# Attention into soft mixture of experts: v and x turned on VectorE, logits by slot, combine in 32-row tiles

## The chip, the core and the metric

The kernel runs on one core of a Trainium2 chip. Time is device time of one execution in microseconds. The core has a matrix engine (PE in the profile), a vector engine (DVE), a scalar engine (ACT), GpSimd (POOL) and a sync engine (SP) that only starts transfers here. Every load of this kernel is started by POOL, every store by SP. Loads read f32 from device memory and write bf16 to on-chip memory (SBUF). Products land in PSUM, eight banks of 512 f32 per partition.

## What is computed

```
q, k, v: 4 batches x 8 heads x 768 positions x 64        (f32)
scores = q @ k.T / 8; causal; heads that are not "retrieval" keep only
         the last 64 positions and the first 4
attn   = softmax(scores) @ v
x      = attn as 3072 tokens x 512 (heads side by side)
logits = x @ phi                        # 3072 x 32 slots, 8 experts of 4 slots
d      = softmax of logits over tokens;  slot_in = d.T @ x        # 32 x 512
per expert e: slot_out = relu(slot_in[e] @ w1[e]) @ w2[e]         # 512 -> 1024 -> 512
c      = softmax of logits over slots;   out = c @ slot_out       # 3072 x 512
```

## The kernel before, in words

Every step is an operation with a rough cost, a priority, dependencies and buffers. A planner (`Plan`) places them by these and then writes each engine's list in that order. On the chip each engine works through its list in order; an instruction that waits holds what stands behind it. POOL's list holds the issues of all loads (`dma`) and the operation VF, so these follow each other.

The 16 pairs of heads (n and n+4 of a batch, four pairs a batch, T = 6.2 us apart in the plan) go through this:

- Loads. `load_part` brings q, k and v of a batch into slots of 8 KB per partition, eleven of them (`S8`), which the expert weights share. Batch 0 comes in three parts per tensor, two of them in 2 KB runs; the others in 8 KB runs. `load_w` brings 16 weights of 1 MB in bf16; the last five go to memory of the attention that has become free (`late_mem`).
- Turns of q, k, v. PE transposes raw chunks into PSUM (lines 415, 439, 461) and DVE or ACT copies them to SBUF (`copy`, lines 218 and 220), so that head dimension lies on partitions. v is turned a second time, back to positions on partitions (V2, line 524, then VB).
- VF (line 541, on POOL): the first four blocks of v times the flag of the head, for score blocks that only retrieval heads keep.
- QK (line 488) in five groups of 1024 columns per pair plus one extra block (QX); exponentials EX on ACT (line 562, pT has two buffers, two pairs); masks MK on DVE (lines 500, 505, 507) for three groups.
- PV (line 621) into one PSUM tile: 42 products of 65 columns a pair, the 65th column being the row sum. From the third block of rows on it reads VF's result.
- NM on DVE (lines 633, 635) divides by the row sum and writes x. PE transposes x (XT, line 647) for the logits, which are taken per token (LG, line 662): 24 products of 32 columns a batch. EL (line 676) is their exponential on ACT.
- DS (line 684) sums x by slot, SA adds the batches up. TE and EE (lines 711, 720) turn the exponentials into expT, four copies of the slots on 128 partitions, for the combine.

After the last pair a chain follows: the last XT, LG, EL, DS, SA; SI (line 768) brings the slot inputs into shape; H (line 781) is the first expert layer, four experts side by side in column tiles of 32; relu (HR), transposes (TH), copies (HE); W2 (line 825) is the second layer, 128 products of 256 columns in tiles of 32, four abreast; CS (line 751) sums the exponentials over tokens by 96 one-column products, RC inverts; SO scales; then 24 tiles of 128 tokens: OM (line 887), a copy with scale by the row sum on ACT or DVE (lines 894, 896), and stores.

Of the kernel before, what the change touches and what calls it, by code (L numbers as in the profile page):

```python
# [10 lines left out]
F32 = mybir.dt.float32  # L11
BF16 = mybir.dt.bfloat16
I32 = mybir.dt.int32
ALU = mybir.AluOpType
# [111 lines left out]
def kernel(  # L126
# [26 lines left out]

    slots = [sb.tile([P, 8 * KB], BF16, name=f"slot{i}") for i in range(11)]
    qk_mem = [sb.tile([P, 12 * KB], BF16, name=f"qk{i}") for i in range(2)]
    pt_mem = sb.tile([P, 20 * KB], BF16, name="pt")
    vx_mem = [sb.tile([P, 3168 + 1024], BF16, name=f"vx{i}") for i in range(2)]
    xv_mem = sb.tile([P, 9 * 1024], BF16, name="xv")
    vfs = [sb.tile([P, 2, 4, 66], BF16, name=f"vf{i}") for i in range(3)]
    ptx = [m[:, 3168:4192].rearrange("p (i n c) -> p i n c", i=2, n=4) for m in vx_mem]  # L160
    xbs = [xv_mem[:, 6144 * i:6144 * i + 3072].rearrange("p (j c) -> p j c", j=6) for i in range(2)]
    xT = sb.tile([P, 4, 768], BF16, name="xT")
    msk = sb.tile([P, H, 640], BF16, name="msk")
    expT = sb.tile([P, 4, 768], BF16, name="expT")
    elg = sb.tile([P, B, 6, NS], BF16, name="elg")
    fm = sb.tile([P, H, 4], BF16, name="fm")
    ident = sb.tile([P, P], BF16, name="ident")
    phf = sb.tile([P, 4, NS], F32, name="phf")
    phi = sb.tile([P, 4, NS], BF16, name="phi")
# [4 lines left out]
    emask = sb.tile([P, 2], F32, name="emask")  # L174
    rcs = sb.tile([P, 1], F32, name="rcs")
    cols = sb.tile([P, 2], BF16, name="cols")
# [4 lines left out]
    edist = sb.tile([P, 640], BF16, name="edist")  # L181
# [3 lines left out]
    vT = xv_mem[:, 3072:6144].rearrange("p (x c) -> p x c", c=128)  # L185
    vbs = [m[:, 0:3168].rearrange("p (n b i d) -> p n b i d", n=4, b=6, i=2) for m in vx_mem]

    tq = xT[:, 0:2, 0:256].bitcast(F32)
    tq = xT.rearrange("p a c -> p (a c)")[:, 0:512].bitcast(F32)
    td = xT.rearrange("p a c -> p (a c)")[:, 512:1024].bitcast(F32)  # L190
    tn = xT.rearrange("p a c -> p (a c)")[:, 1024:1536].bitcast(F32)
    jrow = xT.rearrange("p a c -> p (a c)")[:, 1536:1792].bitcast(F32)
    rne = xT.rearrange("p a c -> p (a c)")[:, 1792:1824].bitcast(F32)
# [8 lines left out]

# [5 lines left out]
    xbf = xT.rearrange("p a c -> p (a c)")  # L208
    hT_t = [xbf[:, 1024 * e:1024 * (e + 1)].rearrange("p (f c) -> p f c", f=8) for e in range(2)]

    pl = Plan({"S8": 11, "QT": 2, "KT": 2, "VT": 1, "VB": 2, "VF": 3, "PT": 2, "PTX": 2, "XB": 2,
               "XT": 1, "SC": 2, "TR": 2, "PV": 1})
    T = 6.2
# [8 lines left out]

    def dma(name, key, nbytes, ndesc, buf, dst, src, deps=()):
        iss = pl.op("issue " + name, {"POOL": 0.62}, key, deps=deps, acq=[buf] if buf else [],
                    emit=lambda o: nc.gpsimd.dma_start(dst(), src))  # L225
        took = ndesc / 16 * 0.0225 + nbytes / 16 / 27170.0
        return pl.op("land " + name, {"DMA": took}, key, deps=[iss], lead=iss_lead[0])

    iss_lead = [2.3]
    raws, lands = {}, {}  # L230
    srcs = {"q": q, "k": k, "v": v}

    def raw_view(buf, p0, p1):
        return slots[buf.slot][p0:p1, :].rearrange("p (i x) -> p i x", i=2)

    def raw_src(x, b, n0, n1):
        a = srcs[x][b].rearrange("(i n) (t s) d -> n t i (s d)", i=2, s=32)[n0:n1]
        return a.rearrange("n t i x -> (n t) i x")


    seq = []
    raw_rel = {}

    def load_part(x, b, part, key):
        if part is None:
            buf = Buf("S8")
            raws[x, b] = buf
            lands[x, b, None] = dma(f"{x}{b}", key, 96 * 2 * 8192, 192, buf,
                                    lambda: raw_view(buf, 0, 96), raw_src(x, b, 0, 4))
        elif part < 2:  # L250
            if (x, b, "s") not in raws:
                raws[x, b, "s"] = Buf("S8")
            buf = raws[x, b, "s"]
            a = srcs[x][b].rearrange("(i n) (t s) d -> n t i (s d)", i=2, s=8)[part]
            lands[x, b, part] = dma(f"{x}{b}.{part}", key, 192 * 2048, 192, buf if part == 0 else None,
                                    lambda: short_view(buf, part), a)
        else:
            raws[x, b] = buf = Buf("S8")
            lands[x, b, part] = dma(f"{x}{b}.{part}", key, 96 * 8192, 96, buf,
                                    lambda: raw_view(buf, 0, 48), raw_src(x, b, 2, 4))  # L260

    def short_view(buf, part):
        return slots[buf.slot][0:96, 1024 * part:1024 * (part + 1)].rearrange("p (i x) -> p i x", i=2)
# [10 lines left out]
    def load_w(i, key, deps=()):  # L274
        if i < NE:
            src = moe_w1[i].rearrange("(di do) f -> di do f", do=4)
        else:
            src = moe_w2[i - NE].rearrange("(fi fo) d -> fi fo d", fo=8)
        wland[i] = dma(f"w{i}", key, 2 << 20, 128, None if i in late_mem else wbuf[i],
                       lambda: w_view(i), src, deps=deps)  # L280


    def tables(o):
        nc.gpsimd.iota(jrow, [[1, 128]], base=0, channel_multiplier=0, allow_small_or_imprecise_dtypes=True)
        nc.gpsimd.iota(pc_i[:, 0:1], [[0, 1]], base=0, channel_multiplier=1)
        nc.gpsimd.iota(tq, [[128, 2], [1, 32], [32, 4]], base=0, channel_multiplier=0,
                       allow_small_or_imprecise_dtypes=True)
# [5 lines left out]
    def key_pos(o):  # L293
        nc.vector.tensor_scalar(pc_i[:, 1:2], pc_i[:, 0:1], 3, 5, op0=ALU.bitwise_and,
                                op1=ALU.logical_shift_left)
        nc.vector.tensor_single_scalar(pc_i[:, 2:3], pc_i[:, 0:1], 2, op=ALU.logical_shift_right)
        nc.vector.tensor_tensor(pc_i[:, 1:2], pc_i[:, 1:2], pc_i[:, 2:3], op=ALU.bitwise_or)
        nc.vector.tensor_copy(pc[:, 1:2], pc_i[:, 1:2])
        nc.vector.tensor_scalar(td, tq, pc[:, 1:2], None, op0=ALU.subtract)
# [3 lines left out]
        nc.vector.tensor_copy(edist[:, 512:640], edist[:, 0:128])  # L303

    def flags(o):
# [3 lines left out]
        nc.vector.tensor_scalar(pc[:, 2:3], pc[:, 1:2], float(n_sink), None, op0=ALU.is_lt)  # L309
# [5 lines left out]
    def head_mask(h):  # L315
        nc.vector.tensor_scalar(msk[:, h, 0:256], edist[:, 0:256], thr[:, 0, h:h + 1], None, op0=ALU.is_lt)
        nc.vector.tensor_scalar(msk[:, h, 256:640], edist[:, 256:640], thr[:, 1, h:h + 1], None, op0=ALU.is_lt)

    def slot_tables(o):

# [4 lines left out]
        nc.vector.tensor_scalar(sum4, jrow[:, 0:NS], pc[:, 3:4], None, op0=ALU.is_equal)  # L325
        nc.vector.tensor_tensor(pc[:, 4:5], pc[:, 4:5], pc[:, 5:6], op=ALU.subtract)
        for e4 in range(2):
            nc.vector.tensor_single_scalar(emask[:, e4:e4 + 1], pc[:, 4:5], 4.0 * e4, op=ALU.is_equal)
        nc.vector.memset(cols[:, 0:1], 1.0)
        nc.vector.memset(cols[:, 1:2], 0.25)  # L330

# [3 lines left out]
    def sp_front(o):  # L335
        nc.sync.dma_start(ri, ri_src)
        pv_ = moe_phi.rearrange("(i n d) s -> i d n s", i=2, n=4)
        for i in range(2):
            nc.sync.dma_start(phf[64 * i:64 * (i + 1)], pv_[i])

    o_sp = pl.op("front", {"SP": 3.5}, -100, emit=sp_front)
    for x in "qk":
        load_part(x, 0, 0, -90)
    o_tab = pl.op("tables", {"POOL": 0.9}, -80, emit=tables)
    load_part("v", 0, 0, -70)
# [606 lines left out]
```

## Time and profile before

| | |
|---|---|
| median of 3 runs | 164.48 us (164.48 to 164.98) |
| span of the profiled execution | 163.6 us, 0.9 below the median |
| PE, PEld busy | 130.3 us (80%), 92.9 us (57%) |
| DVE, ACT busy | 109.4 us (67%), 109.8 us (67%) |
| POOL busy | 39.8 us (24%) |
| loads by POOL (software queue) | 26.22 MB written, 81.2% of 16 engines' span |
| stores by SP (hardware queue) | 6.37 MB, 9.8% |
| last exponential of the attention ends | 122.7 us |
| first product of the first expert layer | 130.1 us |
| first product of the combine | 144.4 us |

PEld is PE loading its stationary operand, which overlaps its products. Issuing a load counts as no busy time on POOL in the shares by engine, though its rows in the order of time have a length. A note in brackets at the end of a row gives the idle time before it and what ended that; "x4" counts instructions that were merged into one row. A group's mean is the time of one instruction from start to end; where instructions overlap, busy time over count is smaller.

### The profile page before, as it was taken

The numbers are of one execution on the slowest core, as the hardware profiler recorded it, in microseconds if no ns is written. First come the engines' busy times: TensorE is split into PE (matmuls) and PEld (weight loads), VectorE is DVE, ScalarE is ACT, GpSimd is POOL, SyncE is SP. The second block draws the span as 40 slices with busy tenths as digits, with TensorE's granted clock in tenths as the row PEclk, the third lists the DMA queues.
The fourth block names the chain that finished last, engine by engine and source line by source line (L and its number), as shares of the span: only waits on it lengthen the run. The fifth ranks groups of instructions, "written<-read, shape, count | busy, mean of one in ns | idle before, by whom it ended". The sixth has DMA issues, their size and how long they took to land.

```text
span 163.6 us, 6186 instructions
## 1 busy us (share of the span) xinstructions
PE 130.3 (80%) x2780; PEld 92.9 (57%) x2780; DVE 109.4 (67%) x228; ACT 109.8 (67%) x133; POOL 39.8 (24%) x59
## 2 busy tenths in 40 slices
PE   0698999999798999988999899699684599978100
PEld 0666777777576676767666676567462246932000
DVE  1899576575787899799799885869975204059400
ACT  3486653288799898898899899979990023068500
POOL 7964311430224202322300243333320000000000
PEclk9999999999999999999999999999998559999955
DMA  2999999999999999999999179999999991019995
GB/s 38 185 197 152 197 210 214 216 218 216 206 216 214 222 220 208 213 211 213 226 215 198 28 118 204 222 218 212 210 222 216 210 216 24 8 62 389 427 423 238
DMA packets 7771, 32.97 MB, mean 201 GB/s; under 512 B 1377, under 2 KB 2529, under 8 KB 5185
## 3 DMA queue, kind: packets, MB, share of 16 engines
q0 software_dynamic: 5760, 26.22, 81.2%
q1 hardware_dynamic: 1984, 6.37, 9.8%
q8 instruction: 21, 0.34, 0.8%
q14 instruction: 6, 0.04, 0.1%
HBM read 52.50 MB, written 6.29 MB: 359 GB/s over the span
## 4 chain that ended last, share of the span: by engine, by line
PE 56%; DVE 15%; ACT 14%; issue 5%; DMA 2%; DVEq 0%; ACTq 0%; POOLq 0%
PE pv L621 15%; PE sc L488 12%; ACT pt L562 10%; PE tr L461 8%; PE sc L781 4%; DVE pt L505 4%; PE tr L439 3%; DVE slot L896 3%; PE tr L647 3%; PE tr L415 2%; DMA slot<-in_q_dram 2%; PE pv L825 2%; DVE xv L635 2%; PE tr L524 2%; PE tr L684 2%
## 5 line engine op out<-in xcount | busy, mean ns | idle before, releaser
L562 ACT ACTIVATE pt<-sc 128x1024 bf16<-128x1024 f32 x80 | 78.7, 1031 | 14.9 <-PE sc L488 13.9
L488 PE MATMUL sc<-qk 64*128 64x256 bf16 (+2 forms) x384 | 35.3, 278 | 3.0 <-ACT pt L562 2.5
L621 PEld LDWEIGHTS <-pt 128*128 128x128 bf16 x640 | 25.4, 101 | 6.9 <-issue 4.8
L621 PE MATMUL pv<-vx,pt 128*128 128x65 bf16 x352 | 28.6, 199 | 0.5 <-DVE pt L507 0.5
L541 POOL TENSOR_TENSOR vf<-vx,fm 128x528 bf16<-128x528 bf16 x16 | 17.8, 1113 | 39.8 <-DVE vx L220 23.6
L621 PE MATMUL pv<-vf,pt 128*128 128x65 bf16 x288 | 23.5, 201 | 0.0
L461 PE MATMUL tr<-ident,slot 96*64 96x96 bf16 x576 | 19.6, 211 | 2.0 <-issue 0.8
L488 PEld LDWEIGHTS <-qk 64*128 64x128 bf16 x384 | 14.0, 97 | 10.6 <-issue 4.6
L461 PEld LDWEIGHTS <-slot 96*64 96x64 bf16 x576 | 15.0, 111 | 6.9 <-issue 5.6
L505 DVE TENSOR_TENSOR pt<-pt,msk 128x512 bf16<-128x512 bf16 x32 | 16.1, 543 | 0.7 <-ACT pt L562 0.6
L635 DVE TENSOR_TENSOR xv<-pv,rs 128x768 bf16<-128x768 f32 x16 | 15.3, 958 | 0.6
L220 DVE COPY qk<-tr 128x768 bf16<-128x768 bf16 x23 | 12.7, 554 | 4.4 <-PE tr L461 3.2
L220 DVE COPY xT<-tr 128x768 bf16<-128x768 bf16 (+1 forms) x15 | 8.6, 573 | 9.4 <-PE tr L804 7.1
L500 DVE TENSOR_TENSOR pt<-pt,msk 128x1024 bf16<-128x1024 bf16 x16 | 11.8, 734 | 2.5 <-ACT pt L562 2.4
L415 PE MATMUL tr<-ident,slot 96*64 96x48 bf16 x192 | 6.9, 228 | 6.6 <-DMA slot<-in_q_dram 5.2
L647 PE MATMUL tr<-ident,xv 128*128 128x128 bf16 x96 | 8.6, 230 | 3.4 <-DVE xv L635 2.4
L225 POOL DMA_DIRECT2D slot<-in_moe_w_dram x11 | 6.3, 573 | 19.7 <-PE tr L461 5.9
L507 DVE TENSOR_TENSOR pt<-pt,msk 128x768 bf16<-128x768 bf16 x16 | 9.4, 587 | 2.2 <-ACT pt L562 1.9
L415 PEld LDWEIGHTS <-slot 96*64 96x64 bf16 x192 | 6.2, 153 | 8.2 <-DMA slot<-in_q_dram 5.2
L647 PEld LDWEIGHTS <-xv 128*128 128x128 bf16 x96 | 6.3, 102 | 5.4 <-DVE xv L635 3.5
L524 PE MATMUL tr<-ident,xv 128*128 128x128 bf16 x96 | 8.6, 232 | 0.4 <-ACT xv L218 0.4
L792 ACT ACTIVATE msk<-sc,emask 128x512 bf16<-128x512 f32 x4 | 2.5, 683 | 7.8 <-PE sc L781 7.8
(106 smaller groups left out, 165.4 us busy)
## 6 DMA issues: line engine op xcount, KB each, us to landing
slot<-in_moe_w_dram POOLq DMA_DIRECT2D x11, 1024.0 KB, 20.6
out_dram<-slot SPq DMA_DIRECT2D x4, 1024.0 KB, 6.9
slot<-in_q_dram POOLq DMA_DIRECT2D x3, 768.0 KB, 30.2
slot<-in_k_dram POOLq DMA_DIRECT2D x3, 768.0 KB, 30.0
slot<-in_v_dram POOLq DMA_DIRECT2D x3, 768.0 KB, 26.2
qk<-in_moe_w_dram POOLq DMA_DIRECT2D x2, 1024.0 KB, 14.9
out_dram<-slot SPq DMA_DIRECT2D x3, 512.0 KB, 3.6
vx<-in_moe_w_dram POOLq DMA_DIRECT2D x1, 1024.0 KB, 15.7
```

Of the source, the lines that this page charges most:

```text
L220: nc.vector.tensor_copy(dst, src)
L415: nc.tensor.matmul(t[64 * i:64 * (i + 1), :, :, s, :], rv[:, i, s, :], idv, start=True, stop=True)
L461: nc.tensor.transpose(t[64 * i:64 * (i + 1), :, s, :], rv[:, i, 8 * c + s, :], ident[0:96, 0:96])
L488: nc.tensor.matmul(scb[sc.slot][:, i, c:c + 128 * nb], kk, qq.rearrange("p b c -> p (b c)"), start=True, stop=True)
L500: nc.vector.tensor_tensor(pT, pT, mh[:, :, 0:512], op=ALU.mult)
L505: nc.vector.tensor_tensor(pv_, pv_, m, op=ALU.mult)
L524: nc.tensor.transpose(t[:, 128 * j:128 * (j + 1)], vT[:, 6 * n + j, :], ident)
L541: eng.tensor_tensor(vfs[VFb[p].slot], vv, mm, op=ALU.mult)
L562: nc.scalar.activation(pTs[PTb[b, n].slot][:, :, 512 * g:512 * (g + 1)], scb[sc.slot], ACT.Exp, scale=scale)
L621: nc.tensor.matmul(pvb[:, h, 65 * i:65 * (i + 1)], lt, rhs, start=(j == 0), stop=(j == i))
L635: nc.vector.tensor_tensor(xo, pvw[:, :, :, 0:64], r.rearrange("p i (j o) -> p i j o", o=1).to_broadcast([P, 2, 6, 64]), op=ALU.mult)
L647: nc.tensor.transpose(t[:, 128 * i:128 * (i + 1)], xv[:, i, 128 * n:128 * (n + 1)], ident)
```

## The change

- v: PE's two turns and their copies go. v is loaded in six pieces (`load_v`), each by four transfers of 32 partitions (or four for two pieces together), and one DVE block transpose per piece (VT, 1024 f32 words per partition, each word two neighbouring bf16) writes it with positions on partitions. VF reads that. v of all batches stays in one memory (`vn`).
- q and k of batch 0 come in two halves of 8 KB runs instead of three parts. q's order within a block of 128 positions changes to match v's; k's copies to SBUF become strided.
- x: PE's turn and its copy become one DVE block transpose per pair (XT, 384 f32 words).
- Logits: taken by slot. phi is laid out as 16 stationary matrices of 128 x 128 with phi's values on diagonal blocks; LG is 16 products of 192 columns a batch. The exponential eT has slots on partitions and gives its own sum over tokens; a DVE transpose (EK) makes the form for DS. TE, EE and the 96 products of CS go; CS is one product.
- Masks: `msk` is 768 columns a head instead of 640, so that each MK is one instruction.
- Experts: HE is four copies per group of four experts, each spreading one expert's 32 columns over 128. W2 becomes 64 products of 512 columns on the full array, so that the slot outputs lie four times, on each 32 partitions. OM uses row tiles of 32 partitions of eT.
- Row sums: six products of 4 columns instead of 24 of one.
- Late weights: 12 and 14 go to the two halves of `vn`, 11 and 13 to q/k memory, 15 to x's memory in three transfers. Weights 14 and 15 wait for the last PV and the last DS. The plan's spacing T is 5.6, and loads, weights and pieces of v are listed in a new order.

```diff
-        lands[x, b, None] = dma(f"{x}{b}", key, 96 * 2 * 8192, 192, buf,
-                                lambda: raw_view(buf, 0, 96), raw_src(x, b, 0, 4))
+    vsrc = v.rearrange("b h (a r s) d -> (b h a) r (s d)", r=4, s=32)
+    def load_v(m, nm, key):
...
+        for r in range(4):
+            src = vsrc[32 * m:32 * (m + nm), r].rearrange("(m g) x -> g m x", m=nm)
+            ls.append(dma(f"v{m}.{r}", key, nm * 32 * 8192, 32 * nm, buf if first and r == 0 else None,
...
-    load_w(0, -30)
-    batch_loads(1, -29)
-    load_w(1, -28)
-    load_w(2, -27)
-    batch_loads(2, -26)
-    for i in (3, 4, 5):
-        load_w(i, -25)
-    batch_loads(3, -24)
-    for i in range(6, 11):
-        load_w(i, -23 + 0.1 * i)
+    batch_loads(1, -30, [(2, 2)])
+    for i in range(0, 3):
+        load_w(i, -27)
+    batch_loads(2, -26, [(4, 2)])
+    for i in range(3, 5):
+        load_w(i, -25)
+    batch_loads(3, -24, [])
+    for i in range(5, 11):
+        load_w(i, -23 + 0.1 * i)
...
+        def emit_vt(o, m=m):
+            s_ = slots[raws["v", m // 2].slot][:, 2048 * (m % 2):2048 * (m % 2 + 1)].bitcast(F32)
+            nc.vector.transpose(vw[:, 32 * m:32 * (m + 1), 0:32].rearrange("p g d -> p d g"),
+                                s_.rearrange("p (s d) -> p d s", d=32))
...
-                nc.tensor.transpose(t[:, 128 * i:128 * (i + 1)], xv[:, i, 128 * n:128 * (n + 1)], ident)
+                nc.vector.transpose(d_, s_)
...
-                    nc.tensor.matmul(trb[lg.slot][:, NS * i:NS * (i + 1)], xT[:, n, 128 * i:128 * (i + 1)],
-                                     phi[:, n, :], start=(n == 0 and i == 0), stop=(n == 3),
+                            nc.tensor.matmul(trb[lg.slot][:, 0:192], phi[:, y, :], xv[:, 2 * n + i, :, par],
+                                             start=(y == 0), stop=(y == 15))
...
-                nc.tensor.matmul(pvb[32 * g:32 * (g + 1), c, 0:256],
-                                 hT_t[e4][:, fo, 32 * g0:32 * (g0 + 1)],
-                                 wv[:, fo, 256 * c:256 * (c + 1)],
+                nc.tensor.matmul(pvb[:, 0, :], hT[:, e, fo, :], wv[:, fo, :],
...
-            nc.tensor.matmul(bank(), out_lhs(gi, r), slot_out, start=True, stop=True)
+            nc.tensor.matmul(bank(), eTf[32 * r:32 * (r + 1), 128 * gi:128 * (gi + 1)],
+                             slot_out[32 * r:32 * (r + 1), :], start=True, stop=True,
+                             tile_position=(32 * r, 0))
...
+    load_w(14, -17, deps=[pv_ops[f"PV.{p}.5"] for p in range(8, 16)] + [vfo[p] for p in range(8, 16)])
+    load_w(15, -16, deps=[pv_ops["DS.3"]] + [pv_ops[f"XT.{p}"] for p in range(12, 16)],
+           parts=((0, 5), (5, 7), (7, 8)))
```

More of the change, by code (lines that the diff above doesn't have):

```diff
@@ L346 @@
[L346 to L358 removed]
+    load_v(0, 1, -70)
@@ L456, in emit_t @@
             def emit_t(o, c=c, tr=tr):
[L457 to L459 removed]
+                t = tr_bf(tr.slot, 32 * nb * (4 // nch)).rearrange("p (x s t) -> p x s t", x=nb, t=4)
+                rv = slots[raw.slot][p0:p0 + rows, :].rearrange("p (i s d) -> p i s d", i=2, d=64)
+                for z in range(per):
+                    s = 4 * (z % 8) + (per // 8) * c + z // 8 if x == "q" else per * c + z
@@ L481, in sc_mms, with vdeps @@
+    def vdeps(b, n):
+        need = set()
+        for i in range(2):
+            for a_ in range(6):
+                need.add((48 * b + 24 * i + 6 * n + a_) // 32)
+        return [vto[m] for m in sorted(need)] + [o_one]
     def sc_mms(sc, b, parts):
```

555 lines of the change are left out of this document (247 added, 308 removed).

## The prediction

> **What bounds the kernel now.** I read the clocks and the span first, then the stretches, then the groups by line, then the order of time on POOL and ACT, and the chain that ended last for the end. The span, then stretches (us; busy PE, PEld, DVE, ACT, POOL, granted clock, DMA share, GB/s written):
>
> ```profile
> core 0: 163.6 us, clock 0.946
> ```
>
> ```profile
> 0.00:5.00 5.00, 0.00 (x0) 0.00 (x0) 1.52 (x8) 1.28 (x1) 3.82 (x12) 1.00 0.47 69
> 5.00:10.00 5.00, 4.47 (x120) 3.73 (x120) 4.76 (x24) 3.44 (x7) 5.00 (x10) 1.00 1.21 184
> 10.00:15.00 5.00, 4.33 (x69) 3.13 (x65) 5.00 (x12) 4.45 (x6) 2.43 (x4) 1.00 1.14 175
> 15.00:20.00 5.00, 4.62 (x86) 3.47 (x86) 3.39 (x15) 2.74 (x4) 1.25 (x2) 1.00 1.12 184
> 20.00:25.00 5.00, 5.00 (x144) 4.04 (x143) 3.52 (x7) 2.31 (x3) 0.64 (x1) 1.00 1.02 209
> 25.00:35.00 10.00, 10.00 (x191) 7.56 (x187) 5.62 (x12) 4.29 (x5) 2.88 (x4) 1.00 1.07 216
> 35.00:45.00 10.00, 8.64 (x208) 6.65 (x204) 7.06 (x15) 8.32 (x12) 2.34 (x3) 1.00 1.02 213
> ...
> 95.00:105.00 10.00, 8.90 (x182) 6.64 (x181) 7.56 (x14) 9.87 (x12) 4.28 (x6) 1.00 1.01 195
> ```
>
> DMA is full from 5 us on. PE is full until 35, ACT is half idle there; later both are near 90%. So three limits take turns: loads and PE early, PE with ACT in the middle, a serial chain at the end. The one execution spans 163.6 us, 0.9 below the median of the runs (164.48); I add that 0.9 back. Now the start, on POOL and ACT:
>
> ```profile
> 12.56 0.56 POOL L225 DMA_DIRECT2D slot<-in_moe_w_dram  x1 [1.77 <-DMA slot<-in_v_dram]
> 13.14 1.08 POOL L541 TENSOR_TENSOR vf<-vx,fm 128x528 bf16<-128x528 bf16 x1
> 29.30 0.56 POOL L225 DMA_DIRECT2D slot<-in_moe_w_dram  x1 [3.25 <-DMA slot<-in_q_dram]
> 29.88 1.08 POOL L541 TENSOR_TENSOR vf<-vx,fm 128x528 bf16<-128x528 bf16 x1
> ```
>
> ```profile
> 9.27 1.94 ACT L562 ACTIVATE pt<-sc 128x1024 bf16<-128x1024 f32 x2
> 30.39 1.02 ACT L562 ACTIVATE pt<-sc 128x1024 bf16<-128x1024 f32 x1 [3.18 <-PE sc L488]
> 120.73 1.94 ACT L562 ACTIVATE pt<-sc 128x1024 bf16<-128x1024 f32 x2
> ```
>
> This is the view that decides. POOL issues every load and also makes vf (VF, the masked v) in one list. Both programs give each load one of eight completion semaphores in turn, so a load's issue waits until the load eight before it has landed. The rows show it: the 14th load (a weight, 12.56) waited for the 6th (a v), the 19th (29.30) for the 11th (q of batch 1); VF follows each at once. So VF, which PV needs from its third block on, queues behind loads.
>
> **Part 1, the order of loads.** v becomes four loads per buffer, which uses up the eight places faster. In the changed program's POOL list 29 loads stand ahead of the first VF: q and k of batch 0 (4), v (8), q and k of batch 1 (2), v (4), three weights, q and k of batch 2, v (4), two weights. The 29th waits for the 21st, which is weight 2. Before, only 14 stood ahead of it, the last waiting on the 6th. What must have landed, in bf16: q,k of batches 0 and 1 3.15 MB, four of the six v pieces 2.10, three weights 3.15, together 8.39 MB. Summing rate by length over the rows above (0.35 + 0.92 + 0.88 + 0.92 + 1.05 + 2.16 + 2.13) the kernel before has moved 8.40 MB at 45.0 us. A load lands later than that mean: the 11th closed 4.2 MB, reached at 25.4 by the same sum, and landed at 29.3, 3.9 late. The 2 KB pieces of batch 0 go (184 and 175 GB/s become about 210, 1 us earlier). So VF starts at 45.0 + 3.9 - 1 = 48; bounds 44 (no lag) and 52 (twice the lag).
>
> Meanwhile ACT can run pairs 0 and 1 only: pT has two buffers, the third pair's first exponential waits for PV of pair 0. PE's list holds that PV, and batch 1's transposes stand behind it. The wait covers all front work (the later first landing, tables, wider head masks, phi's spread, v's transposes 0 to 3): I cost these at nothing. Without the cover ACT would start some 2 us later, since q's and k's first loads double. VF 1.1 us, then 36 of PV's 42 products at the slow pace below (22 in 1.32) 2.2: pair 2 starts on ACT at 51.4. Before it is 30.39, so **+21.0**.
>
> **Part 2, pairs 2 to 15.** Groups by line (busy us, mean ns of one):
>
> ```profile
> L562 ACT ACTIVATE pt<-sc 128x1024 bf16<-128x1024 f32 x80 | 78.7, 1031 | 14.9 <-PE sc L488 13.9
> L635 DVE TENSOR_TENSOR xv<-pv,rs 128x768 bf16<-128x768 f32 x16 | 15.3, 958 | 0.6
> L220 DVE COPY qk<-tr 128x768 bf16<-128x768 bf16 x23 | 12.7, 554 | 4.4 <-PE tr L461 3.2 <-PE tr L439 1.2
> L500 DVE TENSOR_TENSOR pt<-pt,msk 128x1024 bf16<-128x1024 bf16 x16 | 11.8, 734 | 2.5 <-ACT pt L562 2.4
> L507 DVE TENSOR_TENSOR pt<-pt,msk 128x768 bf16<-128x768 bf16 x16 | 9.4, 587 | 2.2 <-ACT pt L562 1.9
> L218 ACT COPY qk<-tr 128x768 bf16<-128x768 bf16 x5 | 4.0, 802 | 1.7 <-PE tr L461 1.7
> L633 DVE RECIPROCAL rs<-pv 128x12 f32<-128x12 f32 x16 | 3.7, 230 | 5.5 <-PE pv L621 5.4
> L584 ACT ACTIVATE vx<-sc 128x1024 bf16<-128x1024 f32 x3 | 3.2, 1058 | 0.0
> L220 DVE COPY expT<-tr 128x768 bf16<-128x768 bf16 x3 | 2.8, 947 | 0.0
> L676 ACT ACTIVATE elg<-tr 128x192 bf16<-128x192 f32 x4 | 1.4, 354 | 4.9 <-PE tr L662 4.9
> ```
>
> The same 70 exponentials remain from there on. Before they take 30.39 to 122.67, 92.3 us. ACT's work in them now: 70 x 0.984 (78.7 over 80, overlaps taken out) = 68.9, the extra columns 0.6 + 3 x 1.06, four logits 1.4, ten q and k copies at 0.80 = 8.0; sum 82.1, or 5.9 per pair. DVE per pair: masks 0.73 + 0.73 + 0.59 (the two halves of L505 become one), NM 1.19, seven q and seven k copies over 14 pairs 0.75 (k's are strided now and are priced by the strided expT row, 0.947), the sums 0.25, x's transpose and v's last two. x's transpose is 384 f32 and has no row: at least 0.23 (the twelve elements of L633), at most 0.96 (768 of L635); by L635's 1.25 ns an element 0.48, I take 0.55. v's 1024 f32 are then 1.3 each (bounds 0.73 and 2.5). DVE 5.0. It saves the copies of v and x, but none of that shows, since ACT is longer. PE, warm against cold:
>
> ```profile
> 17.56 0.54 PE sc L488 x4
> 19.20 1.32 PE pv L621 x22
> 30.35 0.78 PE tr L461 x16
> 34.02 0.46 PE tr L461 x16
> 34.48 0.44 PE tr L524 x6
> 38.75 0.33 PE sc L488 x4
> 47.74 0.79 PE pv L621 x22
> ```
>
> PE loses per pair one of v's raw chunks (0.46), v's second turn (0.44) and x's (0.46 alike), a quarter of the expT turns; phi's block-diagonal products (16 of 192 columns a batch, 1.3 us at W2's pace below, for 24 of 32) give at most 0.3 back. Left per pair are QK 1.85 (five groups, one of six), PV 1.5 (42 products), q and k turns 0.9, logits and slots 0.5: 4.8. So ACT bounds. It reached 0.99 of a stretch (95 to 105) and 0.83 (35 to 45); relieved of PE I take 0.95: 86.4 (82.9 to 99).
>
> But PE starts cold after 20 idle us. At the pace of the rows before 32 us, pair 2 or 3 with batch 1's turns costs PE 2.9 + 2.5 + 3.1 = 8.5 against ACT's 5.9, so 0 to 5.3 us are lost over two pairs; I take 3. The granted clock reads 1.00 there, yet the same four QK took 0.54 and then 0.33. The Trainium skill (TensorE: Matmul & The Clock Gate, Part 1) has the clock released after about 3.4 us of sustained work; by it the loss would be some 1 us and the total 2 lower. The rows speak against it: PE was busy from 17 on and slow until 32. Stage: 89.4, **-2.9**; last exponential at 140.8.
>
> **Part 3, the end.** Rows in order of time; weight loads of PE (PEld) stand for W2:
>
> ```profile
> 124.35 0.96 DVE L635 TENSOR_TENSOR xv<-pv,rs 128x768 bf16<-128x768 f32 x1
> 126.77 0.24 PEld L662 LDWEIGHTS <-xT 128*128 128x128 bf16 x6 [0.92 <-DVE xT L220]
> 130.12 6.38 PE L781 MATMUL sc<-slot,msk 128*32 128x512 bf16 x64 [0.45 <-DVE msk L772]
> 138.52 3.40 PEld L825 LDWEIGHTS <-xT 128*32 128x32 bf16 x128
> 143.28 0.48 DVE L856 TENSOR_SCALAR msk<-pv,rcs 128x256 bf16<-128x256 f32 x1
> 144.38 1.02 PE L887 MATMUL sc<-msk,expT 128*128 128x512 bf16 x4 [0.73 <-ACT msk L854]
> ```
>
> The last NM ends at 125.3, 38.3 before the end. x by transpose takes 0.6 in place of 1.45 to the logits; their last four products cost 0.3 more cold; the eK turn adds 0.35: -0.2. H keeps its 6.38 and W2 starts as late behind it (HE is on DVE for the first expert; four copies per group hide under W2). W2 now spreads each expert over 128 columns: 64 products of 512 columns, none side by side, for 128 of 256 four abreast. 8192 column steps took 3.40, 32768 take 13.6: +10.2 (bounds: 3.4 if they overlapped; 25.6 at H's pace). The Trainium skill's same page (Back-to-back issue gap) gives about 131 ns for N = 512 in a stream; that would make 8.4, and the total 5.2 lower. W2 itself speaks for 213 ns. The column sums leave the path: between W2's end (141.92) and the scaling (143.28) 1.36 becomes 0.15, -1.2. The 32-row combine shortens PE only; evictions and stores from 144.38 to the end stay 19.2. Weights 14 and 15 wait for the last PV and the last slot sums; at 5 us a weight (1.05 MB at 213 GB/s) they land some 12 us after the last NM, W2 wants them at 25: hidden. Tail **+8.8**.
>
> Sum: 163.6 + 21.0 - 2.9 + 8.8 = 190.5, with 0.9 outside 191.4.
>
> **Rivals.** A, faster: VF is not held (weight 2 landing does not gate it, or the list moves on earlier). Then ACT starts some 2 us after today's 9.27, does 82.1 + 12.1 (pairs 0 and 1) at 0.95 without a hole, the last NM ends at 11.5 + 99.2 + 2.6 = 113.3, and the total is 113.3 + 47.1 + 0.9 = 161.3. It decides if VF starts before 48 - 27 = 21 us. For it: an issue itself takes POOL only 0.6. Against it: the two waits shown. B: as forecast, but W2 stays at H's pace after the short pause: +12, 203. For it: H ran all its 6.38 slow; against: W2 before ran fast after the same pause. C: ACT gains nothing in the middle (0.85, transposes at twice my price crowd DVE to 5.7): 201.
>
> **How the numbers follow.** Forecast 0.80 (its own range 182 to 200), A 0.07, B 0.07, C 0.06. 8 in 10 lie in 180 to 204: low end VF at 44, ACT at 0.99, 1 us lost cold; high end covers C and B. 0.3%, 0.5 us, is what a measurement can tell: faster 0.06 (A), same 0.01, slower 0.93.
>
> **What would show it.** POOL: the first VF right behind a weight's issue that waited on a weight, near 48. ACT: a hole of some 20 us after the tenth exponential. After it ACT near 95%, PE near 80% and slow at first. W2 near 13.6 us. Wrong if the first VF starts in the twenties, or if that hole is filled by other pairs.

## The result, and the profile after

The changed kernel takes 189.0 us (188.7 to 189.5, four runs), before 164.5 in the same runs: 1.147 times as long, 95% interval 1.142 to 1.152. The profiled execution spans 187.2 us. Some executions of a variant below are over 1.5% slower than its fastest (in the second and third experiment 176.7 to 181.4 and 176.8 to 181.2 us): medians are of all executions, ratios to before leave the slow ones out, and differences under 2 us are not read from a median alone. Line numbers below are the changed kernel's: VF 511, EX 532, PV 588, QK 487, turns of q and k 435, VT 467, XT 613, MK 500, NM 600 and 602, LG 627, EL 636, H 733, W2 775, OM 814, load issues 230.

First the stretches of the changed kernel, in the columns of the prediction (length; busy PE, PEld, DVE, ACT, POOL; granted clock; DMA share; GB/s). The first row is the middle stage as a whole, from the eleventh exponential to the end of the last:

```profile
49.79:137.24 87.45, 74.25 (x1424) 54.40 (x1422) 67.20 (x108) 79.08 (x90) 22.75 (x27) 0.98 0.79 160
...
25.00:35.00 10.00, 1.89 (x17) 0.92 (x17) 5.73 (x11) 1.83 (x2) 2.89 (x5) 1.00 1.07 217
35.00:45.00 10.00, 0.00 (x0) 0.00 (x0) 2.29 (x3) 0.00 (x0) 1.10 (x2) 1.00 1.04 216
45.00:55.00 10.00, 5.68 (x96) 4.42 (x96) 2.35 (x5) 3.22 (x4) 5.38 (x6) 1.00 1.04 210
55.00:65.00 10.00, 8.87 (x194) 7.19 (x192) 7.40 (x12) 7.78 (x10) 3.27 (x4) 1.00 1.05 217
```

PE and ACT do nothing from 35 to 45 us while the transfer engines are full: a stretch in which PE was 86% busy before is empty. Why is seen on POOL, in order of time (start, length, instructions, and in brackets the idle time ahead and what ended it):

```profile
37.56 0.53 POOL L230 DMA_DIRECT2D slot<-in_v_dram  x1 [3.57 <-DMA slot<-in_moe_w_dram]
42.70 0.56 POOL L230 DMA_DIRECT2D slot<-in_moe_w_dram  x1 [4.61 <-DMA slot<-in_moe_w_dram]
47.62 0.55 POOL L230 DMA_DIRECT2D slot<-in_moe_w_dram  x1 [4.36 <-DMA slot<-in_moe_w_dram]
48.19 3.12 POOL L511 TENSOR_TENSOR vf<-vn,fm 128x528 bf16<-128x528 bf16 x3
```

and on ACT, with the two waits that name what it stood for (engine, tile and line that waited, for whom; us in all, times, longest):

```profile
23.82 3.08 ACT L532 ACTIVATE pt<-sc 128x1024 bf16<-128x1024 f32 x3
49.79 1.02 ACT L532 ACTIVATE pt<-sc 128x1024 bf16<-128x1024 f32 x1 [22.89 <-PE pv L588]
123.22 14.02 ACT L532 ACTIVATE pt<-sc 128x1024 bf16<-128x1024 f32 x15
```

```profile
ACT pt L532 <- PE pv L588: 22.9, 1, 22.9
PE pv L588 <- POOL vf L511: 22.4, 1, 22.4
```

Three loads in a row each wait for a weight to land, VF follows at 48.19, PV waits 22.4 us for VF, ACT 22.9 us for PV. The end, in order of time:

```profile
138.93 0.96 DVE L602 TENSOR_TENSOR xb<-pv,rs 128x768 bf16<-128x768 f32 x1
144.80 6.20 PE L733 MATMUL sc<-slot,msk 128*32 128x512 bf16 x64 [0.39 <-DVE msk L724]
152.93 5.34 PE L775 MATMUL pv<-slot,pt 128*128 128x512 bf16 x24
165.02 1.89 PE L775 MATMUL pv<-xb,pt 128*128 128x512 bf16 x8
167.99 0.40 PE L814 MATMUL sc<-msk,eT 32*128 32x512 bf16 x4 [1.08 <-DVE msk L788]
```

Against before: pair 2 starts at 49.79 instead of 30.39, +19.4; the 70 exponentials from there take 87.45 instead of 92.28, -4.8; from the last exponential to the end of the last NM it is 2.6 both times; from there to the end 47.3 instead of 38.3, +9.0. 163.6 + 19.4 - 4.8 + 9.0 = 187.2, the span.

### The profile page after: what moved, and what is told of

The parts are those of the page before. It is cut to its first block, busy times and chain, and to the rows that moved or that the text cites. A ratio compares the mean times of both kernels' runs of the same rounds, so it can differ in the third digit from the quotient of the medians.

```text
span 187.2 us, 4523 instructions
## 1 busy us (share of the span) xinstructions
PE 119.4 (64%) x1965; PEld 78.0 (42%) x1965; DVE 106.5 (57%) x196; ACT 111.0 (59%) x132; POOL 46.0 (25%) x70
## 4 chain that ended last, share of the span: by engine, by line
PE 24%; DMA 23%; ACT 20%; DVE 19%; issue 6%; POOL 2%; DVEq 0%; ACTq 0%; POOLq 0%
ACT pt L532 15%; DMA slot<-in_moe_w_dram 12%; PE pv L775 7%; DMA slot<-in_q_dram 7%; DVE pt L500 5%; PE pv L588 5%; DMA slot<-in_k_dram 4%; PE sc L733 3%; PE tr L435 3%; DVE slot L825 3%; DVE xb L602 3%; PE sc L487 2%; DVE qk L226 2%; DVE vn L467 2%; PE tr L627 2%
## 5 line engine op out<-in xcount | busy, mean ns | idle before, releaser
L532 ACT ACTIVATE pt<-sc 128x1024 bf16<-128x1024 f32 x80 | 76.9, 1037 | 28.2 <-PE pv L588 22.9
L588 PEld LDWEIGHTS <-pt 128*128 128x128 bf16 x640 | 27.4, 103 | 38.3 <-issue 34.6
L588 PE MATMUL pv<-vf,pt 128*128 128x65 bf16 x288 | 24.9, 203 | 22.4 <-POOL vf L511 22.4
L500 DVE TENSOR_TENSOR pt<-pt,msk 128x1024 bf16<-128x1024 bf16 (+1 forms) x48 | 31.3, 652 | 8.1 <-ACT pt L532 7.7
L588 PE MATMUL pv<-vn,pt 128*128 128x65 bf16 x352 | 31.5, 202 | 6.2 <-DVE xb L602 5.4
L511 POOL TENSOR_TENSOR vf<-vn,fm 128x528 bf16<-128x528 bf16 x16 | 17.9, 1122 | 45.8 <-PE pv L588 45.7
L435 PE MATMUL tr<-ident,slot 96*64 96x96 bf16 (+1 forms) x640 | 21.4, 223 | 10.3 <-DMA slot<-in_q_dram 8.3
L435 PEld LDWEIGHTS <-slot 96*64 96x64 bf16 (+1 forms) x640 | 18.1, 132 | 14.9 <-DMA slot<-in_q_dram 8.8
L487 PEld LDWEIGHTS <-qk 64*128 64x128 bf16 x384 | 15.4, 98 | 16.5 <-issue 10.7
L224 ACT COPY qk<-tr 128x768 bf16<-128x768 bf16 x16 | 12.9, 804 | 12.0 <-PE tr L435 11.9
L467 DVE STREAM_TRANSPOSE vn<-slot 128x1024 f32<-128x1024 f32 x6 | 12.2, 2030 | 7.9 <-DMA slot<-in_v_dram 7.9
L602 DVE TENSOR_TENSOR xb<-pv,rs 128x768 bf16<-128x768 f32 x16 | 15.3, 958 | 0.6
L230 POOL DMA_DIRECT2D slot<-in_v_dram x16 | 8.4, 526 | 13.4 <-DMA slot<-in_k_dram 4.7
L613 DVE STREAM_TRANSPOSE xT<-xb 128x384 f32<-128x384 f32 x16 | 9.2, 576 | 0.3
## 6 DMA issues: line engine op xcount, KB each, us to landing
qk<-in_moe_w_dram POOLq DMA_DIRECT2D x2, 1024.0 KB, 10.3
```

The source lines that it names most:

```text
L224: nc.scalar.copy(dst, src)
L435: nc.tensor.transpose(t[64 * i:64 * (i + 1), :, z, :], rv[:, i, s, :], ident[p0:p0 + rows, p0:p0 + rows])
L467: nc.vector.transpose(vw[:, 32 * m:32 * (m + 1), 0:32].rearrange("p g d -> p d g"), s_.rearrange("p (s d) -> p d s", d=32))
L487: nc.tensor.matmul(scb[sc.slot][:, i, c:c + 128 * nb], kk, qq.rearrange("p b c -> p (b c)"), start=True, stop=True)
L500: eng.tensor_tensor(pT, pT, msk[:, n::4, c0:c1], op=ALU.mult)
L511: nc.gpsimd.tensor_tensor(vfs[VFb[p].slot], vh[:, b, n, :, 0:4, :], mm, op=ALU.mult)
```

## The experiments

Each median stands beside before's in runs on the same chip, 164.5 to 165.0.

### VF ahead of the weights

In the diffs, `move` stands for taking the operations named out of the planner's finished order and putting them back, in their own order, behind another one.

```diff
     order = pl.run()
+    # in the order of writing, and so in POOL's list
+    move("issue w0 w1 w2 q2 k2 v4.*", behind="VF.2")
+    move("issue w3", behind="VF.3"); move("issue w4", behind="VF.4")
```

> Only POOL's list is changed: VF.0 to VF.2 come behind the 18th load (the last v piece of the first two v buffers) and the clearing of phi, ahead of the weights; weight 3 goes behind VF.3 and weight 4 behind VF.4. The same transfers, the same work. Theory (the list holds VF): VF.0 starts near 21.6, where the clearing of phi ends in the changed kernel (19.83 + 1.82); the second v buffer's transposes end at 22.4, so VF.1 and VF.2 are done by 25; the tenth exponential ends near 27, so pair 2 starts between 27 and 30 instead of 49.79, and the median falls from 189.0 by 20 to 23, to 166 to 169. Rival (the transfers hold it anyway: full transfer queues, q and k late): pair 2 still starts past 45 and the median stays within 3 of 189. Rival (the hold moves): VF.3 stands behind the 27th load, which went out at 37.56, so if that now ends last, pair 5 waits instead, VF.3 starts past 38 with ACT idle before it, and only some 10 us are won (179).

172.5 us (172.5 to 173.1), 1.047 [1.041, 1.053] of before. In order of time, POOL, ACT, DVE and PE of this run:

```profile
21.51 3.12 POOL L511 TENSOR_TENSOR vf<-vn,fm 128x528 bf16<-128x528 bf16 x3
28.18 2.16 ACT L532 ACTIVATE pt<-sc 128x1024 bf16<-128x1024 f32 x2 [2.42 <-PE sc L487]
42.98 1.02 ACT L532 ACTIVATE pt<-sc 128x1024 bf16<-128x1024 f32 x1 [0.58 <-PE sc L487]
32.44 2.04 DVE L467 STREAM_TRANSPOSE vn<-slot 128x1024 f32<-128x1024 f32 x1 [0.96 <-issue]
34.78 1.99 DVE L467 STREAM_TRANSPOSE vn<-slot 128x1024 f32<-128x1024 f32 x1
37.07 0.96 DVE L602 TENSOR_TENSOR xb<-pv,rs 128x768 bf16<-128x768 f32 x1
38.08 0.49 PE L588 MATMUL pv<-vn,pt 128*128 128x65 bf16 x6 [5.18 <-DVE xb L602]
```

VF starts at 21.51 (expected 21.6) and pair 2 at 29.32: the row at 28.18 merges the tenth exponential and the eleventh, which is the first of pair 2 (expected 27 to 30). 16.5 us are won with the same transfers and the same work, so the order of POOL's list is the cause of the hold. VF of pair 3 starts past 38 (38.03), as the third forecast had it, but nothing waits for it there: PV of pair 3 starts at 49.60. The median is 3.5 to 6.5 us short of the expectation. A second hold that I had not named stands at that place: PV of pair 1 waits 5.18 us for the first NM, which stands on DVE behind two v transposes of 2.0 us each. Whether it is what is missing is asked further down.

### Two loads behind VF

```diff
+    move("issue w3 w4", behind="VF.2")     # 27 loads ahead of VF instead of 29
```

> Two POOL entries alone change places: the loads of weights 3 and 4 (the 28th and 29th) go behind VF.2, so 27 loads stand ahead of VF.0 instead of 29. Theory (a load waits for the load eight before): the 27th went out at 37.56, when the 19th had landed, so VF.0 starts at 38.1 instead of 48.19, pair 2 near 39.7 instead of 49.79, and the median is 189.0 - 10.1 = 179, with an error of 2. Rival (the wait is for the engine's or the queue's free room in bytes, or VF waits for its v): two loads in 29 are 7% of the list, VF.0 moves by under 2 us and the median stays at 187 to 189.

179.7 us (176.7 to 181.4). POOL and ACT in order of time:

```profile
37.34 0.53 POOL L230 DMA_DIRECT2D slot<-in_v_dram  x1 [3.52 <-DVE vn L467]
37.89 3.12 POOL L511 TENSOR_TENSOR vf<-vn,fm 128x528 bf16<-128x528 bf16 x3
39.50 1.02 ACT L532 ACTIVATE pt<-sc 128x1024 bf16<-128x1024 f32 x1 [12.76 <-PE pv L588]
```

Two of 29 places move VF by 10.3 us (48.19 to 37.89) and pair 2 by 10.3 (49.79 to 39.50). A list that were merely 7% shorter would have moved it by 2. The 27th load went out at 37.34, in the changed kernel at 37.56. (The bracket names the v transposes on DVE, which ended at 37.14; in the changed kernel and in the first experiment the same issue, at 37.56 and 37.48, is put down to a weight's landing, and the 19th load is weight 0.) What counts is which landing the last load ahead of VF waits for. The span is 12.3 us shorter than the changed kernel's (174.9 for 187.2): 10.3 by the shift, and 2.0 behind it, to which I return under Part 2 below.

### W2 in column groups

```diff
-    nc.tensor.matmul(pvb[:, 0, :], hT[:, e, fo, :], wv[:, fo, :], ...)
+    g = fo % 4
+    nc.tensor.matmul(pvb[32*g:32*(g+1), 0, :], hT[:, e, fo, 0:32], wv[:, fo, :],
+                     ..., tile_position=(0, 32*g))
...
+    copy(slot_prt, pvb[:, 0, :])                         # bf16, half on ACT, half on DVE
+    nc.tensor.matmul(pvb[:, 1, :], ident_rep, slot_prt)  # adds four groups, repeats them
```

> The second expert product (W2) alone is changed back to four column groups: 64 products of 32 slots by 512, four side by side, instead of 64 of 128 by 512 one after the other; the four partial sums are then copied to bf16 and added and repeated by one product with a 0/1 matrix; the copies of h turned (HE) write 32 columns instead of 128. Theory (W2 was mis-chosen, 13.54 us on the path): W2 takes 3.4 as before, the added copy and product take some 0.5 + 0.3 + 0.5 of waits, so the tail is 8.5 to 9 shorter: 180 to 180.5. Rival (W2 waits for something else, the last weights that landed near 152 us or a cold TensorE): W2 still spans 7 or more, and the median stays above 183.

180.45 us (176.8 to 181.2). PE in order of time (H, W2 from its first to its last, the adding product at line 791, OM at 825):

```profile
145.57 6.35 PE L734 MATMUL sc<-slot,msk 128*32 128x512 bf16 x64 [0.38 <-DVE msk L725]
153.94 1.48 PE L777 MATMUL pv<-slot,pt 128*32 128x512 bf16 x24
156.98 0.60 PE L777 MATMUL pv<-xb,pt 128*32 128x512 bf16 x8
158.54 0.38 PE L791 MATMUL pv<-msk,ident_rep 128*128 128x512 bf16 x1 [0.96 <-DVE msk L227]
160.00 0.40 PE L825 MATMUL sc<-msk,eT 32*128 32x512 bf16 x4 [1.08 <-DVE msk L799]
```

W2 takes 3.6 instead of 14.0 us from first to last row, and the added copy and product put 2.4 between its end and OM where the changed kernel has 1.1. The weights did not hold it. From the first H to the first OM it is 14.4 us instead of 23.2, so W2's form is a loss of 8.8 us by the two profiles; the medians give 8.5. The same two edits of the tail, this one and the next, won 8.6 and 8.8 in two further pairs of kernels (198.3 to 189.7 and 181.7 to 172.9, the latter with a price of the planner changed as well).

### The exponential without its sums

```diff
-    nc.scalar.activation(eT, logits, ACT.Exp, accum_out=esum[:, b:b+1])
+    nc.scalar.activation(eT, logits, ACT.Exp)
+    nc.vector.reduce_sum(esum[:, b:b+1], eT[:, b])
```

> The exponential of the logits (EL) no longer adds up its rows; a DVE reduction of 192 elements behind it makes the sums instead. In the changed kernel EL takes 1014 ns and a read of the sum 498 ns, where before's took 354. Theory (the summing costs it): EL falls to 0.35 to 0.5 and the read is gone, 1.1 us on the path at the end and up to 1.1 three times in the middle, where ACT is 90% busy: 185 to 188. Rival (the permuted write, 4 elements apart in 6 by 8 by 4, costs it): EL stays near 1.0 and only the 0.5 of the read goes: 187.5 to 188.7. Rival (both off the path): 189.

188.5 us (188.2 to 189.5). Groups by line (busy us, mean ns of one):

```profile
L636 ACT ACTIVATE eT<-tr 128x192 bf16<-128x192 f32 x4 | 4.0, 1010 | 6.0 <-PE tr L627 6.0
L646 DVE TENSOR_REDUCE esum<-eT 128x1 f32<-128x192 bf16 x4 | 1.2, 310 | 0.0
```

EL keeps its 1.01 us without the summing; only the read of the sum (0.498 each) goes. So the sum is not what makes EL three times as long as before's 0.354. The write in another order (each result goes eight elements behind the one before) is the other difference that I see between the two, but no run took it away alone.

### Transposes of v behind the first normalisations

> The first experiment's kernel (VF.0 to VF.2 ahead of the weights, 172.5) with two more steps moved: in DVE's list the transposes of the third and fourth v pieces (VT.2, VT.3, needed from pair 4 and pair 8 on) come behind XT.1 and XT.2 instead of ahead of the first normalisation (NM.0); in POOL's list VF.4 follows VT.2, and the loads of q and k of batch 3 and of weight 5 follow VF.5. In the first experiment PE stood 5.18 us from 32.9 to 38.08 for NM.0, which stood behind VT.2 (32.44, 2.04) and VT.3 (34.78, 1.99). Theory (the rest of the gap to before lies in DVE's list, at twice the price I took for a v transpose): the wait goes, and the median falls by 4 to 5.5, to 167 to 168.5. Rival (the next thing in DVE's list, the eight copies of phi, 3.07 us from 27.7, or the late q of batch 1 holds PE instead): 170 to 172.5. Rival (VF.4 and pair 4 become late by it): above 172.5.

> The kernel of the run before this one with the column groups of W2 and the exponential without sums. If the three gains lie in different stretches they add: 167.5 to 168.5, less 8.5 for W2 (189.0 to 180.45), less 0.5 for the exponential (189.0 to 188.5): 158 to 160, 3 to 4% under before's 165. If the earlier W2 then waits for the last weights (they landed some 12 us after weight 15 was issued), 161 to 164.

198.3 us (196.9 to 198.7) and, with the tail's two edits, 189.7 (188.0 to 191.7). Neither answers its question. I had put the load of q of batch 3 ahead of VT.3 though both use one buffer; so VT.3 turned q instead of the fourth piece of v, and waited for that load (the longest wait of DVE):

```profile
DVE vn L467 <- DMA slot<-in_q_dram: 28.2, 1, 28.2
```

It shows only that one late entry of DVE's list costs about what it waits: 28.2 us there, 25.8 in the time (198.3 against 172.5). Put right:

```diff
+    move("VT.2", behind="XT.0"); move("VT.3", behind="XT.1")
+    move("issue q3", behind="VT.3"); move("issue k3 w5", behind="the last turn of k of batch 1")
```

> The question of the run with label e5 again, which did not answer it: there the transpose VT.3 stood in the lists behind the load of q of batch 3 that takes its buffer, so it waited for that load and took the wrong data. Here, on top of the first experiment's order (172.5), VT.2 comes behind XT.0 and VT.3 behind XT.1 in DVE's list, and the loads of q and k of batch 3 and of weight 5 come behind them. Theory (what is left of the start's loss is DVE's list: NM.0 behind two v transposes of 2.0 each, PE idle 5.18): the wait on NM.0 falls to about 1, the median to 167.5 to 169. Rival (DVE is simply full between 20 and 40 us, 90% busy, so the same work delays the next step by as much): 171.5 to 173.

173.7 us (173.1 to 175.3), no gain over 172.5. The wait itself is gone, by the waits of this run:

```profile
PE pv L588 <- DVE xb L602: 5.4, 10, 1.1
```

but the stretches behind it, of the run with VF ahead and then of this one, read:

```profile
36.00:44.00 8.00, 5.92 (x104) 5.04 (x105) 7.15 (x11) 1.82 (x2) 2.22 (x3) 0.59 1.02 213
44.00:52.00 8.00, 6.34 (x135) 4.58 (x130) 5.60 (x10) 7.50 (x9) 2.33 (x3) 0.99 1.06 217
```

```profile
36.00:44.00 8.00, 6.40 (x119) 5.04 (x119) 7.93 (x11) 4.39 (x6) 3.07 (x4) 0.66 1.03 215
44.00:52.00 8.00, 6.66 (x85) 4.60 (x84) 5.41 (x9) 6.20 (x7) 1.19 (x3) 0.50 1.04 212
```

DVE works 7.93 of 8 us from 36 to 44, as the rival had it; and TensorE's granted clock is at half from 44 to 52 where it was full, so PE, with fewer instructions (85 for 135), is as busy. The second has a part of its own. PV of pair 1 starts 4.35 us earlier than in the first experiment (33.73 for 38.08), PV of pair 4 only 0.66 (53.68 for 54.34). Of what is lost, 1.2 us go between PV of pair 3 and PV of pair 4 (5.92 us for 4.74), where DVE works 3.64 of 6 us and turns no v. How the rest divides between DVE's list and the clock these runs do not show.

### The planner told of the eight places

```diff
         land = pl.op("land " + name, ...)
+        places.append(land)
+        if len(places) > 8:
+            iss.deps.append(places[-9])     # the load eight before has landed
```

> Changed kernel; the planner alone is told that a load goes out only when the load eight before it has landed (in the order in which they are written down), and it makes every list anew. Theory (the order came from a planner that does not know this limit): it puts VF.0 behind the 15th load, which in the changed kernel went out at 15.04, so VF.0 starts near 16, pair 2 between 26 and 30, and the median is 165 to 170. Rival (the planner's prices, not the limit, made the order late; a v transpose priced 1.15 takes 2.03): holds of 4 us and more remain on PE in the first 50 us and the median stays at 171 to 176. Rival (no effect): 187 to 191.

> The planner with the eight places, a v transpose priced 2.0 instead of 1.15, the column groups of W2 and the exponential without sums. If the planner's order is as good as the one made by hand: 157 to 160. If the lists then hold elsewhere: 161 to 166.

181.7 us (181.5 to 183.0) and, with the tail's two edits and the new price, 172.9 (172.6 to 174.6). The first is 7.3 us under the changed kernel and 9 us worse than the order by hand; neither time lies in any of its forecasts. VF.0 starts at 15.39 and the eleventh exponential at 27.8, as expected; other holds take the place of the first. The longest wait of PE in the first of the two, and two of its stretches:

```profile
PE tr L440 <- DMA slot<-in_q_dram: 11.9, 3, 6.8
```

```profile
60.00:70.00 10.00, 7.95 (x148) 5.83 (x147) 9.21 (x12) 7.08 (x8) 2.32 (x3) 0.70 1.02 214
...
90.00:100.00 10.00, 6.23 (x106) 4.54 (x103) 3.05 (x5) 4.60 (x6) 0.00 (x0) 0.50 0.97 200
```

In the second PE waits 11.9 us at once for a k. The planner moved q and k of later batches behind weights, PE waits for them in its own list, and the half clock returns again and again. It knows the limit now, but counts places in the order in which loads are written down, not in the order in which it issues them; whether that is what goes wrong was not tried.

### All that helped, together

> The run before this one, with the copies of phi (3.07 us on DVE near 27.7) moved to ACT behind the tenth exponential, the column groups of W2 and the exponential without sums. If they add: 168 - 8.5 - 0.5 - up to 2 for phi = 157 to 160, under before's 164.5 to 165. If an earlier start of the middle stretch brings a lower granted clock there (0.79 to 0.87 between 30 and 50 us in the first experiment), 160 to 163. If the middle is the same and the tail waits for the last weights: 162 to 165.

165.8 us (164.6 to 169.4), 1.006 [1.002, 1.009] of before, and above all three forecasts. The tail's gain is there (173.7 to 165.8 is 7.9); the start is not better, and W2 waits for no weight. What moving phi's copies did was not taken apart. Stretches:

```profile
44.00:52.00 8.00, 6.19 (x77) 4.29 (x78) 5.53 (x8) 4.50 (x5) 1.51 (x2) 0.50 1.03 210
52.00:58.00 6.00, 5.58 (x53) 4.05 (x50) 2.90 (x5) 3.68 (x6) 2.16 (x4) 0.53 1.08 215
```

Here the half clock lasts through nearly all of these 14 us.

### TensorE kept busy in its holds

```diff
     # PV.0, before its third block
+    for _ in range(300):
+        nc.tensor.matmul(pvb[:, 0, 390:512], ident, ident[:, 0:122])
```

> Changed kernel with 300 products of 128 by 122 without use put on PE ahead of PV.0's third block, in the stretch where PE stands still (27 to 49.3), into columns of PV's bank that nothing reads. They measure what the idle stretch costs afterwards through a slow TensorE (my term: 3 us of 89.4, bounds 0 to 5.3). At 0.055 us each, warm, they end near 45, 4 us ahead of VF.0. Theory (3 us): the 36 products of PV.0 take under 1.5 us instead of 2.14, the transposes behind it 0.53 per 16 instead of 0.85, and the median falls by 2 to 4, to 185 to 187. Rival (the slow stretch lies beside ACT's own work): 188.5 to 189.5. Rival (more work on TensorE brings a lower granted clock later): 190 or more.

188.2 us (185.3 to 189.4), no difference that this spread can show. It missed its aim:

```profile
26.69 17.96 PE L582 MATMUL pv<-ident 128*128 128x122 bf16 x300
49.03 0.21 PE L590 MATMUL pv<-vf,pt 128*128 128x65 bf16 x1 [4.38 <-POOL vf L511]
51.10 0.85 PE L435 MATMUL tr<-ident,slot 96*64 96x96 bf16 x16
```

```profile
54.00:56.00 2.00, 2.00 (x44) 1.79 (x41) 0.56 (x1) 1.96 (x3) 0.00 (x0) 0.50 1.10 219
```

The work ended 4.38 us ahead of VF, and that was enough: sixteen transposes behind it take 0.85 us, as long as behind the full hold, and the granted clock reads 0.50 until 57 with PE at work throughout (the last row is one stretch of it). The term of 3 us stays unmeasured by this run.

> The first experiment's kernel (172.5) with the column groups of W2 and the exponential without sums (172.5 - 8.5 - 0.5 = 163.5 if they add), and with work without use that keeps TensorE busy where it stood still: the sixteen transposes of the third piece of q of batch 1 are made nine times over, so that they last from 32.4 to some 36.6 of the hold that ended at 38.08, and in the tail 25, 14, 8 and 5 products of 128 by 122 stand ahead of the last logits (LG), DS, SI and the first expert product (H), in the waits of 1.93, 1.1, 0.54 and 0.38 there. In the first experiment the granted clock was 0.50 from 38 to 44 behind the first hold and from 126 to 132 in the tail, with H at 5.44 for 60 products. Theory (a hold of some 4 us halves the clock for 6 to 14 us behind it, and this is a loss of its own beside the hold): the granted clock stays at 1.00 at both places, the ten QK products behind the hold take some 0.55 instead of 1.04, H takes 3 to 3.6, and the median is 157.5 to 161, under before's 164.8. Rival (the half clock comes by itself or comes 10 us later): granted clock still 0.50 for as long in all, and 163 to 165. Rival (ACT and DVE set the pace at the start, so a faster TensorE buys nothing there): the clock stays up, H is shorter, and only the tail's 2 to 3 us are won: 160.5 to 161.5.

165.45 us (163.7 to 168.9), 1.003 [0.999, 1.007] of before: no difference from before, and in none of the three forecasts. PE in order of time (QK behind the hold, H, OM):

```profile
42.94 0.61 PE L492 MATMUL sc<-qk 64*128 64x256 bf16 x10
129.51 3.64 PE L744 MATMUL sc<-slot,msk 128*32 128x512 bf16 x64
142.44 0.61 PE L835 MATMUL sc<-msk,eT 32*128 32x512 bf16 x4 [1.08 <-DVE msk L809]
```

At the start the clock did not stay up: in the three stretches of 2 us from 38 to 44 it reads 0.82, 0.50 and 0.82, where it was at half from 38 to 44 in the first experiment. Ten QK products take 0.61 instead of 1.04, but the hold itself ends later, with NM.0 (39.05 for 38.08), and the exponential behind them starts at 43.44 instead of 42.98. So what a full clock is worth there stays open. In the tail H takes 3.64 us, and in every other run here 5.6 to 6.4. OM starts 9.0 us earlier than in the first experiment (151.49), yet the span is only 6.8 shorter (170.6 to 163.8): 2.2 us are lost behind OM in this execution. W2 takes 4.9 us instead of the 3.6 of the third experiment and waits twice, 0.25 each, for pieces of the last weight. From the end of the last NM to OM it is 18.2 us, in the run of all together 19.4, so 1.2 of the 2.8 us by which H is shorter are left. No run has this kernel without the extra work, so what that is worth in the median is not shown.

## Why the prediction was right, point by point

- **Part 1, VF held by loads: right, and shown.** VF.0 at 48.19 (48 predicted), by exactly the chain named; removing the cause removes the hold (first experiment), and shifting two loads shifts it by the landing they wait for (second). That the time came out to 0.2 us is partly luck. By the same sum the changed kernel too had moved 8.4 MB at 45.0 us, so the 1 us that the longer runs of the loads were to win did not come (166 and 175 GB/s from 5 to 15 us, where I had put 210); and the last load was issued 2.6 us behind that, not 3.9. The two errors nearly cancel. Pair 2 started at 49.79, not 51.4: the 36 products took 2.1 us as predicted (49.32 to 51.46), but the exponential did not wait for all of them. It started 0.5 us after the first. So the part of PV.0 that counts was mis-sized, 0.5 for 2.2: +19.4 for +21.0.
- **Part 2: the sum near, its parts off against each other.** 87.45 for 89.4. ACT had 79.1 us of work, not 82.1: its groups add up to 84.3, but they overlap by 5.2, and I had taken overlaps out among the exponentials alone. Its idle time was 8.4, where 4.3 + 3 were predicted. By the stretches, ACT was idle 4.2 of the first 15.2 us (49.79 to 65, 3.22 + 7.78 busy) and 4.2 of the other 72.2, a share of 0.94 for my 0.95. So the start cost some 3.3 us beyond the rest, for the 3 that I took for a slow PE. The run that was to measure this ended its filling too early, but the second experiment bears on it. Behind its hold PE ran the same products at the slow pace for some 3 us only (sixteen transposes take 0.85 us at 41.09 and 0.53 at 42.41; in the changed kernel they still take 0.85 at 56.03). From the eleventh exponential to the end of the last it takes 85.46 us, 2.0 less than the changed kernel, and the 2.0 are won in ACT's waits for PE at the start (1.47, 0.20 and 0.21 us for 1.47, 0.52 and 1.97). So some 5 us of slow PE cost ACT 2.0: the mechanism is there, within my bounds of 0 to 5.3, and the 3 is not contradicted.
- **Prices of the transposes.** Groups of the changed kernel:

```profile
L467 DVE STREAM_TRANSPOSE vn<-slot 128x1024 f32<-128x1024 f32 x6 | 12.2, 2030 | 7.9 <-DMA slot<-in_v_dram 7.9
L613 DVE STREAM_TRANSPOSE xT<-xb 128x384 f32<-128x384 f32 x16 | 9.2, 576 | 0.3
L636 ACT ACTIVATE eT<-tr 128x192 bf16<-128x192 f32 x4 | 4.1, 1014 | 4.6 <-PE tr L627 4.5
L636 ACT ACTIVATION_READ_ACCUMULATOR eT<-tr 128x1 f32 x4 | 2.0, 498 | 0.0
```

  x's is right (0.58 for 0.55); v's is 2.03 for 1.3, within its bounds (0.73 to 2.5) but not where I put it. In the changed kernel this costs little, since two of the four early ones fall into the hold. Once the hold is gone they are what PE waits for next (5.18 us in the first experiment), though putting them elsewhere won nothing. EL at 1.0 and its read at 0.5 were not foreseen at all.
- **Part 3: right in sum and in its main term.** 47.3 from the last NM to the end, 47.1 predicted. W2 14.0 us from first to last row and 13.6 predicted; with 64 products that is 218 ns each, near the 213 of before's W2. The Trainium skill (TensorE: Matmul & The Clock Gate, Back-to-back issue gap) gives about 131 ns for N = 512 in a stream; this trace does not agree. From the last NM to H it is 4.9 us for before's 4.8, where 0.2 less was predicted. H keeps its pace (6.20 for 6.38), OM to the end is 19.2 as before, and the last weights were hidden. The third experiment takes W2's form out: 10.3 us less in W2, 1.3 more behind it, 8.8 in all with the other steps up to OM.
- **Rivals.** A's condition (VF before 21) did not hold; made true by hand in the first experiment, with the tail unchanged, it gave 172.5 and not 161.3. The last NM ends at 123.5 there instead of 113.3. The first exponential comes at 13.02, not 11.5 (1.5 late), and up to the last one ACT idles 17.1 us where a share of 0.95 allowed 5.0 (9.0 of them from 28.18 to 50), with 3.4 us less work than I had counted. A had counted with ACT alone. B and C did not occur.
- **Outside the span** stand 1.8 us between the profiled span and the median, for the 0.9 taken over from before. In all the forecast of 191.4 was 2.4 us high: 1.6 from Part 1, 1.9 from Part 2, less 0.2 from Part 3 and 0.9 here.

## What to carry to other kernels

Where one engine's list holds both the issues of loads and a small operation that others need, count the loads ahead of that operation against the number that may be under way, and see which landing the last one waits for: two entries were worth 10 us here. A planner that does not know such a limit writes an order that looks free and is not, and after the first hold is cut the next list holds instead (here DVE's, with a transpose priced 1.15 us in the plan and measured at 2.03). Reordering that list alone won nothing here. Replacing four narrow products side by side by one wide one in a serial tail is paid in full: 32 slots spread over 128 columns took 14 us for 3.6.

## What was not expected of the hardware

- A 32 x 32 block transpose on DVE cost 2.03 us for 1024 f32 per partition read with a stride, 2.0 ns an element, against 1.5 for x's 384 (0.576 us).
- TensorE's half clock. A wait of 4.38 us left it as slow as one of 22.4 (0.85 us per sixteen transposes in both), which agrees with the Trainium skill (TensorE: Matmul & The Clock Gate, Part 1: half rate after an idle window of about 3.4 us). How long it then lasts differs from run to run. The same section has a busy window of about 3.4 us release it. The second experiment agrees: PE ran without a pause from 39.02 and was at full pace after some 3 us. The changed kernel does not: the same products in the same order ran at half pace for 8 us from 49.32, with PE at work for all 5.68 us up to 55; nor does the run with 300 products (granted clock 0.50 to 57, PE at work from 49.03 on). With short waits in between, the granted clock stayed at half for all of 44 to 52 us with PE busy for 6.66 of 8 us, and from 44 to 57 in the run of all together. So short waits are not needed to keep it there, and what decides the length is open.
- The granted clock of the changed kernel reads 1.00 from 45 to 65 us although its pace was half until about 57 (sixteen transposes 0.85 us at 56.03, 0.70 at 57.47); in the run with 300 products it reads 0.50 at that pace. The pace of like instructions is the safer reading.
- H ran at half clock in both kernels (granted clock 0.50 in most of it, 6.38 and 6.20 us); with TensorE kept busy through the waits of 0.4 to 1.9 us ahead of it, it took 3.64 at 1.00.
